# First modulation loads as eight row blocks, and keys that begin when all of shift and scale is there

## The chip, the cores and the metric

The kernel runs on one core of one Trainium2 chip. The metric is device time in microseconds (us) of one execution. The span that the profile shows runs from the first to the last instruction and is about 2 us shorter than that time. Every kernel has one profiled execution, so a number read from a trace is one sample.

## The reference

A transformer block with adaptive layer norm: 2048 tokens, width 1024. The part that matters is the beginning.

```python
mod = (_silu(c) @ w_mod).reshape(c.shape[0], 6, 1, -1)      # c: 1 x 1024, w_mod: 1024 x 6144, bf16
sa, ca, ga, sb, cb, gb = ...                                # six rows of 1024
h = _layernorm(x, axis=-1) * (1 + ca) + sa
x = x + ga * _A_ref(h, A_wqkv, A_wo)                        # linear attention: keys, values, queries from h
h = _layernorm(x, axis=-1) * (1 + cb) + sb
x = x + gb * _B_ref(h, ...)                                 # SwiGLU
```

The first keys need `h`, so they need the shift `sa` and the scale `ca`: two matrix-vector products ("matvecs") with the first 2048 columns of `w_mod`, 4.19 MB. Hidden unit 128 cc + p sits in chunk cc, partition p.

## The kernel before

x arrives in tiles of 128 tokens (256 KB). Shift (q = 0) and scale (q = 1) are loaded by halves b of the hidden units; the first half is enough for chunks 0 to 3, so the keys start on these while the second half is still loading.

```python
wme = [[big("wme", [DC, NB]) for _ in range(2)] for _ in range(2)]
def load_mod(b, q, lo, hi):
    nc.sync.dma_start(out=wme[b][q][:, :, lo:hi], in_=wm_v[:, :, q * D + b * NB + lo:q * D + b * NB + hi])
load_mod(0, 1, 0, NB)            # 1 MB in 1024 rows of 1 KB
load_mod(0, 0, 0, NB)
load_k(0); load_k(1); load_x(STC - 1, nc.sync); load_k(2); load_k(3)     # (shortened) 256 KB each
load_mod(1, 1, 0, NB)
load_mod(1, 0, 0, NB // 2)       # rows of 512 B
load_k(4); load_k(5)
load_mod(1, 0, NB // 2, NB)
load_k(6); load_k(7)
# ... cut ...
def mod_block(b, q, lo, hi):     # 128 columns by 128 rows at a time: a matmul with one moving column
    for i in range(lo, hi):
        col = q * DC + 4 * b + i
        for j in range(DC):
            mm(mod_ps[:, col:col + 1], lhsT=wme[b][q][:, j, i * P:(i + 1) * P],
               rhs=scT[:, j:j + 1], start=(j == 0), stop=(j == DC - 1))
    # ... copied to saT or, plus one, to ca1T
# ... cut: c, silu, layer norm and transposes of tiles 0 to 2, keep-warm matmuls in between ...
for lo, hi in ((0, 1), (1, 4)):
    mod_block(0, 0, lo, hi)
    for cc in range(lo, hi):
        modulate(hT, cc, ca1T, saT, 0, H)
k_mms(0, gs, accs, 0, 4)                  # 24 key matmuls: six groups, chunks 0 to 3
xn3 = ln1_norm(*ln1_stats(0, 3), dve=True)
pe_transpose_tile(hT, xn3, 3, DC // 2)    # ScalarE copies chunks 4 to 7 from PSUM, VectorE 0 to 3
for cc in range(4):
    modulate(hT, cc, ca1T, saT, H, SCW)
mod_block(1, 1, 0, 4)
# ... cut: keys of tile 3, the other half of the modulation and chunks 4 to 7, interleaved ...
```

`keep_warm(acc, n)` issues n matmuls of 512 columns whose result nobody reads, so that TensorE doesn't stand idle.

## Time and profile before

| | before |
|---|---|
| time, three executions | 839.66 us median (838.86 to 839.79) |
| span of the profiled execution (none of the three; it took 838.63 us) | 836.6 us |
| TensorE busy | 829.8 us (99%) |
| last modulation load that the first key needs has landed | 13.25 us |
| the first keys' own weights have landed | 13.94 us |
| first key matmul | 14.50 us |
| first value matmul ("V") | 31.95 us |

The page of the kernel before: the span, TensorE's busy time, and in 40 slices of 21 us TensorE's busy share and its granted clock (the share of full speed that the throttle allowed it) in tenths, the DMA share in tenths, and GB/s.

```profile
span 836.6 us, 11355 instructions
PE 829.8 (99%) x4701; PEld 380.7 (46%) x4701; DVE 307.6 (37%) x598; ACT 170.1 (20%) x255; POOL 60.9 (7%) x165
...
PE   8999999999999999999999999999999999999998
...
PEclk9999999999999999999999999999999999999999
DMA  9894890029997446337434173672505529710011
GB/s 311 305 253 100 254 213 2 13 68 239 366 243 262 151 151 207 120 99 229 150 102 151 45 221 100 201 239 62 189 1 127 188 69 322 241 60 0 13 64 51
```

TensorE bounds the kernel from the second slice on. DMA is near full in the first three slices and in some later ones, but there TensorE's digit stays at 9. From the start of the first V matmul to that of the last matmul of all, the trace has 801.32 us; with the same work after V, a saving before V should count one to one.

The chain of waits of the kernel before, for its first 60 us (start, us, what):

```profile
2.98 10.27 DMA wme<-in_w_mod_dram
...
13.30 0.37 PE mod_ps L98 x8
...
13.69 0.17 DVE saT L264
...
13.90 0.74 PE mod_ps L98 x24
14.64 5.20 PE acc L98 x24
```

The first keys wait for the second modulation load, then for matvecs, a copy and a modulation pass.

The timeline of TensorE in the same trace (start, us busy; in brackets the idle time before and what ended it):

```profile
14.50 5.34 PE L98 MATMUL acc<-wk,hT 128*128 128x512 bf16 x24
19.68 0.61 PE L101 MATMUL tp<-ident,xn 128*128 128x128 bf16 x8
20.13 0.94 PE L98 MATMUL mod_ps<-scT,wme 128*128 128x1 bf16 x32
21.78 0.61 PE L98 MATMUL acc<-wk,hT 128*128 128x512 bf16 x2 [0.71 <-DVE hT L218]
...
25.94 0.54 PE L98 MATMUL mod_ps<-scT,wme 128*128 128x1 bf16 x16
26.34 5.76 PE L98 MATMUL acc<-wk,hT 128*128 128x512 bf16 x25
```

The key stretch holds matvecs of the second half and a wait for tile 3. Its length, and the length of V, are in the windows view (from:to, length, busy time of each engine, then granted clock, DMA share and GB/s):

```profile
core 0: us, PE busy (x) PEld busy (x) DVE busy (x) ACT busy (x) POOL busy (x), PEclk, DMA share, GB/s
0.00:14.50 14.50, 11.99 (x119) 6.17 (x120) 7.54 (x20) 5.77 (x6) 3.13 (x12) 1.00 0.88 297
14.50:31.95 17.45, 16.51 (x143) 8.33 (x140) 8.83 (x28) 4.20 (x7) 2.17 (x35) 1.00 1.08 372
31.95:45.93 13.98, 13.98 (x66) 6.33 (x65) 10.90 (x28) 9.28 (x14) 3.22 (x8) 1.00 0.51 171
```

### The profile page before, as it was taken

The numbers are of one execution on the slowest core, as the hardware profiler recorded it, in microseconds if no ns is written. First come the engines' busy times: TensorE is split into PE (matmuls) and PEld (weight loads), VectorE is DVE, ScalarE is ACT, GpSimd is POOL, SyncE is SP. The second block draws the span as 40 slices with busy tenths as digits, with TensorE's granted clock in tenths as the row PEclk, the third lists the DMA queues.
The fourth block names the chain that finished last, engine by engine and source line by source line (L and its number), as shares of the span: only waits on it lengthen the run. The fifth ranks groups of instructions, "written<-read, shape, count | busy, mean of one in ns | idle before, by whom it ended". The sixth has DMA issues, their size and how long they took to land.

```text
span 836.6 us, 11355 instructions
## 1 busy us (share of the span) xinstructions
PE 829.8 (99%) x4701; PEld 380.7 (46%) x4701; DVE 307.6 (37%) x598; ACT 170.1 (20%) x255; POOL 60.9 (7%) x165
## 2 busy tenths in 40 slices
PE   8999999999999999999999999999999999999998
PEld 4444444444444444444444444444444444444444
DVE  5755554587413324521111344222114431111122
ACT  3455343334211111101111110111110101111000
POOL 2011211111130001100000010000001100000000
PEclk9999999999999999999999999999999999999999
DMA  9894890029997446337434173672505529710011
GB/s 311 305 253 100 254 213 2 13 68 239 366 243 262 151 151 207 120 99 229 150 102 151 45 221 100 201 239 62 189 1 127 188 69 322 241 60 0 13 64 51
DMA packets 127668, 129.34 MB, mean 155 GB/s; under 512 B 33920, under 2 KB 109184, under 8 KB 127104
## 3 DMA queue, kind: packets, MB, share of 16 engines
q1 hardware_dynamic: 123568, 115.36, 45.7%
q0 software_dynamic: 4048, 13.25, 5.4%
q8 instruction: 37, 0.61, 0.3%
q14 instruction: 15, 0.12, 0.1%
HBM read 108.53 MB, written 12.72 MB: 145 GB/s over the span
## 4 chain that ended last, share of the span: by engine, by line
PE 97%; DMA 1%; DVE 1%; SPq 0%; ACT 0%; issue 0%
PE acc L98 89%; PE a_ps L98 7%; DMA wme<-in_w_mod_dram 1%; PE kvp L98 1%; PE modr L98 0%; PE den L98 0%; PE mod_ps L98 0%; DVE hT L218 0%; SPq L120 0%; DVE wo L528 0%; PE wf L98 0%; DVE pq L273 0%; ACT eb L270 0%; ACT hT L226 0%; PE tp L101 0%
## 5 line engine op out<-in xcount | busy, mean ns | idle before, releaser
L98 PE MATMUL acc<-h2T,wgu 128*128 128x512 bf16 x1792 | 387.6, 379 | 0.0
L98 PEld LDWEIGHTS <-wgu 128*128 128x128 bf16 x1792 | 175.3, 98 | 211.3
L98 PE MATMUL acc<-wd,gu 128*128 128x512 bf16 (+2 forms) x924 | 196.1, 373 | 0.0
L597 DVE TENSOR_TENSOR gu<-acc,e 128x512 bf16<-128x512 f32 x112 | 77.5, 692 | 299.2 <-PE acc L98 296.5
L596 ACT ACTIVATE e<-acc 128x512 f32<-128x512 f32 x112 | 66.9, 597 | 374.8 <-PE acc L98 374.8
L98 PEld LDWEIGHTS <-gu 128*128 128x128 bf16 x924 | 89.3, 98 | 104.4
L98 PEld LDWEIGHTS <-hT 128*128 128x128 bf16 x512 | 49.2, 98 | 60.4 <-DVE hT L218 1.5
L618 DVE TENSOR_TENSOR e<-acc,gb_bc 128x512 f32<-128x512 f32 (+2 forms) x33 | 22.3, 675 | 131.9 <-PE acc L98 131.9
L98 PE MATMUL acc<-wk,hT 128*128 128x512 bf16 x256 | 57.6, 379 | 0.8 <-DVE hT L218 0.7
L98 PE MATMUL a_ps<-wo,pq 128*128 128x512 bf16 x256 | 57.4, 379 | 0.0
L98 PE MATMUL acc<-hT,wq 128*128 128x512 bf16 x256 | 56.8, 379 | 0.0
L98 PE MATMUL acc<-wv,hT 128*128 128x512 bf16 x256 | 55.9, 379 | 0.0
L270 ACT ACTIVATE eb<-acc 128x512 bf16<-128x512 f32 x64 | 37.9, 595 | 66.2 <-PE acc L98 63.1
L215 ACT ACTIVATE xn<-x,nmr,rstd 128x1024 bf16<-128x1024 f32 x16 | 19.8, 1240 | 126.3 <-POOL nmr L213 126.3
L565 POOL DMA_DIRECT2D x_scratch<-x x16 | 9.7, 608 | 418.5 <-DVE x L558 418.5
L98 PEld LDWEIGHTS <-pq 128*128 128x128 bf16 x256 | 25.0, 98 | 30.2
L98 PEld LDWEIGHTS <-wq 128*128 128x128 bf16 x256 | 24.6, 98 | 29.8 <-issue 0.9
L271 DVE TENSOR_SCALAR eb<-eb 128x512 bf16<-128x512 bf16 x64 | 18.4, 292 | 49.0 <-ACT eb L270 49.0
L558 DVE TENSOR_TENSOR x<-a_ps,x_sb 128x512 f32<-128x512 f32 x32 | 22.1, 691 | 7.9 <-PE a_ps L98 7.8
L199 POOL TENSOR_TENSOR rstd<-veps,neg_half 128x1 f32<-128x1 f32 x32 | 17.9, 559 | 75.3 <-DVE veps L197 72.9
L308 ACT CAST v<-acc 128x512 bf16<-128x512 f32 x32 | 18.3, 582 | 23.1 <-PE acc L98 23.0
L621 DVE TENSOR_TENSOR ob<-e,x1r 128x512 bf16<-128x512 f32 (+2 forms) x33 | 22.3, 675 | 1.0
(70 smaller groups left out, 263.1 us busy)
## 6 DMA issues: line engine op xcount, KB each, us to landing
wgu<-in_B_w_gate_dram SPq DMA_DIRECT2D x28, 1024.0 KB, 7.9
wgu<-in_B_w_up_dram SPq DMA_DIRECT2D x28, 1024.0 KB, 8.7
x_sb<-in_A_x_dram SPq DMA_DIRECT2D x32, 256.0 KB, 6.8
wml<-in_w_mod_dram SPq DMA_DIRECT2D x8, 1024.0 KB, 8.7
x_scratch<-x POOLq DMA_DIRECT2D x16, 512.0 KB, 3.0
x1r<-x_scratch SPq DMA_DIRECT2D x31, 256.0 KB, 2.8
wd<-in_B_w_down_dram SPq DMA_DIRECT2D x7, 1024.0 KB, 6.0
rbc<-rden_scratch POOLq DMA_DIRECT2D x16, 256.0 KB, 5.4
```

What stands on the lines that cost most here:

```text
L98: return tc.keep_in_program_order(nc.tensor.matmul(out, lhsT=lhsT, rhs=rhs, start=start, stop=stop))
L199: nc.gpsimd.tensor_tensor(out=rstd[:, 0:n], in0=veps[:, 0:n], in1=neg_half[:].to_broadcast([P, n]), op=ALU.pow)
L215: nc.scalar.activation(out=dst, in_=src, func=ACT.Identity, bias=nmr[:], scale=rstd[:, 0:1])
L270: nc.scalar.activation(out=e[:], in_=acc, func=ACT.Exp)
L271: nc.vector.tensor_scalar(out=e[:], in0=e[:], scalar1=1.0, scalar2=PHI_EPS, op0=ALU.min, op1=ALU.add)
L308: nc.scalar.copy(out=v[:, t * D + nb * NB:t * D + (nb + 1) * NB], in_=acc[:])
L558: nc.vector.tensor_tensor(out=x1[:, ns], in0=a_ps[:], in1=x_t[:, ns], op=ALU.add)
L565: nc.gpsimd.dma_start(out=x1_dram[st * P:(st + 1) * P, :], in_=x1[:])
L596: nc.scalar.activation(out=sg[:], in_=ps[0][:], func=ACT.Silu)
L597: gm = nc.vector.tensor_tensor(out=guT[sc][f // GPT][:, f % GPT, :], in0=ps[1][:], in1=sg[:], op=ALU.mult)
L618: nc.vector.tensor_tensor(out=yt, in0=y_ps, in1=gb_bc[:, ns], op=ALU.mult)
L621: nc.vector.tensor_tensor(out=ob, in0=yt, in1=x1r, op=ALU.add)
```

## The change

The intent: load `w_mod` by blocks of 128 rows with 4 KB in a row, which moves faster than rows of 1 KB and 512 B; accumulate the matvecs block by block under the loads, so that only the last block is exposed; and then run the keys without matvecs between them. The price is that 4.19 MB instead of 2.10 MB stand ahead of the first key.

```diff
-    wme = [[big("wme", [DC, NB]) for _ in range(2)] for _ in range(2)]
-    ... load_mod, and its calls between the key loads
+    wme = [big("wme", [2, 2 * D]) for _ in range(DC // 2)]
+    for j in range(DC):
+        nc.sync.dma_start(out=wme[j // 2][:, j % 2, :], in_=wm_v[:, j, 0:2 * D])
+    for cc in range(4):
+        load_k(cc)
     load_x(STC - 1, nc.sync)
+    for cc in range(4, DC):
+        load_k(cc)
...
+    def mod_block(j):
+        for col in range(2 * DC):
+            mm(mod_ps[:, col:col + 1], lhsT=wme[j // 2][:, j % 2, col * P:(col + 1) * P], rhs=scT[:, j:j + 1],
+               start=False, stop=(j == DC - 1 and col == 2 * DC - 1))
...
+        mm(mod_ps[:, 0:2 * DC], lhsT=ident[:], rhs=base[:], start=True, stop=False)   # shift 0, scale 1
...
+        keep_warm(spare, 5)
+        mod_block(0)
+        ... blocks 1 to 4, with tiles 0 to 2 and keep-warm matmuls between them
+        for j in range(5, DC):
+            keep_warm(spare, 4)
+            mod_block(j)
+        nc.vector.tensor_copy(out=sca[:], in_=mod_ps[:, 0:2 * DC])
+        for cc in range(DC):
+            modulate(hT, cc, ca1T, saT, 0, H)
+        k_mms(0, gs, accs, 0, 6)
         xn3 = ln1_norm(*ln1_stats(0, 3), dve=True)
+        tp3 = pe_transpose_tile(xn3)
+        for cc in range(DC):
+            nc.vector.tensor_scalar(out=hT[:, cc, H:SCW], in0=tp3[:, cc, :], ...)     # modulated from PSUM
+        k_mms(0, gs, accs, 6, DC)
         gs7, accs7 = k_groups[6:7], [acc_b("acc")]
+        k_mms(0, gs7, accs7)
         gs8, accs8 = k_groups[7:8], [acc_b("acc")]
         k_mms(0, gs8, accs8)
```

More of the change, by code (lines that the diff above doesn't have):

```diff
@@ L127 @@
     wk = [big("wk", [4, D]), big("wk", [4, D])]
-    wme = [[big("wme", [DC, NB]) for _ in range(2)] for _ in range(2)]
-    def load_mod(b, q, lo, hi):
-        nc.sync.dma_start(out=wme[b][q][:, :, lo:hi], in_=wm_v[:, :, q * D + b * NB + lo:q * D + b * NB + hi])
+    wme = [big("wme", [2, 2 * D]) for _ in range(DC // 2)]
     def load_k(cc):
         nc.sync.dma_start(out=wk[cc // 4][:, cc % 4, :], in_=wqkv_v[:, cc, D:2 * D])
-    load_mod(0, 1, 0, NB)
-    load_mod(0, 0, 0, NB)
-    load_k(0)
-    load_k(1)
+    for j in range(DC):
+        nc.sync.dma_start(out=wme[j // 2][:, j % 2, :], in_=wm_v[:, j, 0:2 * D])
+    for cc in range(4):
+        load_k(cc)
     load_x(STC - 1, nc.sync)
-    load_k(2)
-    load_k(3)
-    load_mod(1, 1, 0, NB)
-    load_mod(1, 0, 0, NB // 2)
-    load_k(4)
-    load_k(5)
-    load_mod(1, 0, NB // 2, NB)
-    load_k(6)
-    load_k(7)
+    for cc in range(4, DC):
+        load_k(cc)
     def load_w(view, lo, name):
@@ L167 @@
     nc.vector.memset(neg_half[:], -0.5)
+    base = const.tile([P, 2 * DC], BF16, name="base")
+    nc.vector.memset(base[:, 0:DC], 0.0)
+    nc.vector.memset(base[:, DC:], 1.0)
     scT = const.tile([P, DC], BF16, name="scT")
     sc32 = const.tile([P, DC, 32], BF16, name="sc32")
-    saT = const.tile([P, DC], F32, name="saT")
-    ca1T = const.tile([P, DC], F32, name="ca1T")
+    sca = const.tile([P, 2 * DC], F32, name="sca")
+    saT, ca1T = sca[:, 0:DC], sca[:, DC:2 * DC]
     sbT = const.tile([P, DC], F32, name="sbT")
@@ L219, in modulate, with pe_transpose_tile @@
                                 scalar2=biasT[:, cc:cc + 1], op0=ALU.mult, op1=ALU.add)
-    def pe_transpose_tile(hT, xn, t, split):
+    def pe_transpose_tile(xn):
         tp = acc_b("tp", (DC, P), BF16)
@@ L224, in pe_transpose_tile @@
             transpose(tp[:, cc, :], xn[:, cc * P:(cc + 1) * P])
-        if split < DC:
-            nc.scalar.copy(out=hT[:, split:DC, t * P:(t + 1) * P], in_=tp[:, split:DC, :])
-        nc.vector.tensor_copy(out=hT[:, 0:split, t * P:(t + 1) * P], in_=tp[:, 0:split, :])
+        return tp
     hTs = {}
@@ L251, in ln1 @@
             ln1_norm(*ln1_stats(sc, t))
-    def mod_block(b, q, lo, hi):
-        for i in range(lo, hi):
-            col = q * DC + 4 * b + i
-            for j in range(DC):
-                mm(mod_ps[:, col:col + 1], lhsT=wme[b][q][:, j, i * P:(i + 1) * P],
-                   rhs=scT[:, j:j + 1], start=(j == 0), stop=(j == DC - 1))
-        cs = slice(4 * b + lo, 4 * b + hi)
-        src = mod_ps[:, q * DC + 4 * b + lo:q * DC + 4 * b + hi]
-        if q == 1:
-            nc.vector.tensor_scalar_add(out=ca1T[:, cs], in0=src, scalar1=1.0)
-        else:
-            nc.vector.tensor_copy(out=saT[:, cs], in_=src)
+    def mod_block(j):
+        for col in range(2 * DC):
+            mm(mod_ps[:, col:col + 1], lhsT=wme[j // 2][:, j % 2, col * P:(col + 1) * P], rhs=scT[:, j:j + 1],
+               start=False, stop=(j == DC - 1 and col == 2 * DC - 1))
     last_phi = [None]
@@ L425 @@
         mod_ps = acc_b("mod_ps")
-        mm(mod_ps[:, 0:DC], lhsT=c_sb[:], rhs=ident[0:DC, 0:DC], start=True, stop=True)
-        keep_warm(spare, 10)
-        nc.scalar.activation(out=scT[:], in_=mod_ps[:, 0:DC], func=ACT.Silu)
+        mm(mod_ps[:, 2 * DC:3 * DC], lhsT=c_sb[:], rhs=ident[0:DC, 0:DC], start=True, stop=True)
+        mm(mod_ps[:, 0:2 * DC], lhsT=ident[:], rhs=base[:], start=True, stop=False)
+        nc.scalar.activation(out=scT[:], in_=mod_ps[:, 2 * DC:3 * DC], func=ACT.Silu)
@@ L429 @@
         xns = [ln1_norm(*ln1_stats(0, t)) for t in range(3)]
-        pe_transpose_tile(hT, xns[0], 0, DC)
-        keep_warm(spare, 3)
-        pe_transpose_tile(hT, xns[1], 1, DC)
-        keep_warm(spare, 2)
-        mod_block(0, 1, 0, 4)
-        pe_transpose_tile(hT, xns[2], 2, DC // 2)
-        keep_warm(spare, 4)
-        for lo, hi in ((0, 1), (1, 4)):
-            mod_block(0, 0, lo, hi)
-            for cc in range(lo, hi):
-                modulate(hT, cc, ca1T, saT, 0, H)
-        k_mms(0, gs, accs, 0, 4)
@@ L442 @@
-        xn3 = ln1_norm(*ln1_stats(0, 3), dve=True)
-        pe_transpose_tile(hT, xn3, 3, DC // 2)
-        for cc in range(4):
-            modulate(hT, cc, ca1T, saT, H, SCW)
-        mod_block(1, 1, 0, 4)
-        gs7, accs7 = k_groups[6:7], [acc_b("acc")]
-        k_mms(0, gs7, accs7, 0, 2)
-        for cc in (4, 5):
-            mod_block(1, 0, cc - 4, cc - 3)
-            modulate(hT, cc, ca1T, saT)
-            if cc == 4:
-                k_mms(0, gs7, accs7, 2, 4)
-        k_mms(0, gs + gs7, accs + accs7, 4, 5)
@@ L455, with turn @@
-        k_mms(0, gs[0:4], accs[0:4], 5, 6)
-        mod_block(1, 0, 2, 4)
-        for cc in (6, 7):
-            modulate(hT, cc, ca1T, saT)
-        k_mms(0, gs[4:6] + gs7, accs[4:6] + accs7, 5, 6)
-        k_mms(0, gs + gs7, accs + accs7, 6, 8)
+        def turn(t):
+            tp = pe_transpose_tile(xns[t])
+            nc.vector.tensor_copy(out=hT[:, :, t * P:(t + 1) * P], in_=tp[:])
+        keep_warm(spare, 5)
+        mod_block(0)
+        keep_warm(spare, 2)
+        mod_block(1)
+        turn(0)
@@ new lines @@
+        keep_warm(spare, 1)
+        mod_block(2)
+        keep_warm(spare, 1)
+        turn(1)
+        keep_warm(spare, 2)
+        mod_block(3)
+        keep_warm(spare, 2)
+        turn(2)
+        mod_block(4)
+        for j in range(5, DC):
[5 more added lines that the diff above has]
+        k_mms(0, gs, accs, 0, 6)
+        xn3 = ln1_norm(*ln1_stats(0, 3), dve=True)
@@ L461 @@
+        tp3 = pe_transpose_tile(xn3)
+        for cc in range(DC):
+            nc.vector.tensor_scalar(out=hT[:, cc, H:SCW], in0=tp3[:, cc, :], scalar1=ca1T[:, cc:cc + 1],
+                                    scalar2=saT[:, cc:cc + 1], op0=ALU.mult, op1=ALU.add)
+        k_mms(0, gs, accs, 6, DC)
+        gs7, accs7 = k_groups[6:7], [acc_b("acc")]
+        k_mms(0, gs7, accs7)
         gs8, accs8 = k_groups[7:8], [acc_b("acc")]
```

## The prediction

> **What bounds the kernel now.** TensorE is busy 829.8 of 836.6 us (page, part 1); the chain of waits is 97% PE. In the V phase, from 31.95 us, the timeline shows a matmul every 0.217 us without a break. So the change, which touches only the first 32 us, pays only by letting V start earlier. Up to there DMA holds PE: the windows view shows DMA share about 1.0 from 7 to 35 us, and the chain has a 10.27 us wait for a modulation load that ends at 13.25 us. The first key matmul runs at 14.50 us; V starts 17.45 us later: 13.9 us of key matmuls, 1.9 of matvecs, 0.6 of transposes, about 1.1 of waits.
>
> **What the change does.**
> - Bytes ahead of the first key: x (0.79 MB) and 4.19 MB of modulation instead of 2.10: about 5.1 us more.
> - Row size: the trace's packet records have medians of 46 ns for 1 KB, 84 for 2 KB, 159 for 4 KB; on 16 engines 356, 390, 412 GB/s. This agrees with the Trainium skill, "DMA: Bandwidth & Descriptors", section "Why small descriptors are slow" (fixed overhead per packet; here about 8 ns). All 4.19 MB are 64 packets on each engine, 10.2 us, against about 12.3 in 1 KB and 512 B rows.
> - Skew: the landing semaphores show the first modulation load ending between 7.45 and 10.28 us, five engines late, and that lateness stays. SP's queue stood 3.7 us behind 1,024-row loads, with DMA share 0.78 at 4 to 6 us. Blocks of 128 rows should fill this dip and cut part of the skew.
> - Matvecs: the same 128 (about 0.45 us per 16). Seven blocks hide under loads; the last is exposed. With four keep-warm matmuls (0.95 us) a block is 1.4 us against 1.27 us of load, so PE may slip 0.1 us a block.
> - Key stretch after: 64 matmuls (13.9 us) and eight transposes (0.5 us), no matvec, no wait: a chunk of keys takes 1.3 us against 0.67 us per 256 KB load; tile 3 needs about 3 us of normalisation within the 7.8 us of 36 matmuls, and loses two copies.
> - Evacuation gets two groups of cover instead of one; off the path.
>
> **Sum.** x has landed on most engines at 4.6 us; plus 10.2 us of blocks, 14.8; receipt and remaining skew (0.4 to 2.5 us) say 1.3: last block at 16.1 us (15.0 to 17.3). Then 16 matvecs 0.4, copy and modulate 0.83 (measured from last matvec to first key): first key at 17.3 us. Plus 14.4: V at 31.7 us against 31.95, then the same work. The change moves 2.8 us of loading ahead of the keys and takes 3 us of matvecs and waits out of them: nearly a wash.
>
> **Predicted time:** 839.4 us, 8 in 10 between 838.0 and 840.9. Faster by over 2%: 0.005; within 2%: 0.99; slower: 0.005.
>
> **What would show it.** First key at 17.3 us; from there to V 14.4 us without idle; V start within 1.2 us of 31.95; over 380 GB/s from 4 us; 4 KB packets at 159 ns; last block at 16.1 us with skew under 2.8 us; clock 1.00 throughout; V and all later phases of equal length.
>
> **What would make it wrong.** Engines as late as before or later (first key at 18.5, 1 us slower); no skew (up to 1.3 us faster); blocks come unevenly, PE idles and the clock drops ("TensorE: Matmul & The Clock Gate", section "HAM oscillation": gaps over about 3.4 us; before, no gap is so long and the clock stays 1.00); tile 3 or a key load arrives late and the key stretch waits.

## The result

| | before | after |
|---|---|---|
| time, four executions each | 839.26 us median (838.16 to 839.79) | 839.61 us median (839.43 to 841.25) |
| ratio, 95% interval | | 1.001 (0.9993 to 1.0028) |
| span of the profiled execution | 836.6 us | 839.4 us |
| spans of the three others | | 837.6, 837.7, 837.8 us |

A ratio is the mean time of one kernel's fast runs over that of the other's of the same rounds, so it isn't quite the ratio of the medians quoted. The change is within 2%. The same kernel in a later session (experiment 1) came out at 839.6 against 838.04 us, ratio 1.0017 with an interval from 1.0005 to 1.003: slower, by about 1.5 us (1.4 by the ratio, 1.6 by the medians).

The page of the changed kernel:

```profile
span 839.4 us, 11369 instructions
PE 831.8 (99%) x4708; PEld 381.6 (45%) x4708; DVE 307.5 (37%) x597; ACT 168.8 (20%) x253; POOL 60.6 (7%) x165
...
DMA  9793990029999545527434174571504529710011
GB/s 346 268 242 89 274 202 13 3 76 211 348 252 271 177 151 188 138 77 250 150 101 151 41 217 107 192 247 56 195 1 138 177 69 322 236 63 0 16 60 51
```

TensorE is as busy as before. DMA moves 346 GB/s instead of 311 in the first slice, as intended. What came of it shows in the chain of waits:

```profile
6.05 11.40 DMA wme<-in_w_mod_dram
17.44 0.05 issue
17.49 0.57 PE mod_ps L98 x16
...
18.16 0.18 DVE sca L435
...
18.36 0.39 DVE hT L211
...
18.80 9.30 PE acc L98 x36
```

The last block lands at 17.44 us, and the first key runs at 18.80 us, 4.3 us later than before (its own weights landed at 18.10). The timeline of TensorE:

```profile
14.88 0.54 PE L98 MATMUL mod_ps<-scT,wme 128*128 128x1 bf16 x16
15.28 1.02 PE L98 MATMUL acc<-sel 128*128 128x512 bf16 x4
17.49 0.55 PE L98 MATMUL mod_ps<-scT,wme 128*128 128x1 bf16 x16 [1.19 <-DMA wme<-in_w_mod_dram]
18.80 9.30 PE L98 MATMUL acc<-wk,hT 128*128 128x512 bf16 x36 [0.76 <-DVE hT L211]
```

Thirty-six key matmuls took 9.30 us here, 0.258 us each, instead of 0.217. The clock tells why; the windows view:

```profile
0.00:18.80 18.80, 14.89 (x190) 8.34 (x191) 7.84 (x22) 6.36 (x6) 3.13 (x12) 0.98 0.91 341
18.80:34.43 15.63, 15.63 (x72) 7.07 (x73) 9.84 (x28) 3.37 (x6) 2.17 (x35) 0.91 1.05 386
34.43:48.41 13.98, 13.98 (x66) 6.35 (x65) 9.44 (x26) 9.50 (x13) 3.21 (x8) 1.00 0.35 86
```

The granted clock was 0.5 from 18.18 to 21.59 us, one piece of 3.41 us in the trace's clock records. It began 0.69 us after the end of the idle piece of 1.19 us; the second one, of 0.76 us from 18.04 to 18.80, lies mostly inside it. So keys ran at half rate from 18.80 to 21.59 us, which costs half of 2.79, 1.4 us: the first 36 took 7.94 us in the later trace of the same kernel (a_again), not 9.30. It belongs to this execution: the three others had a clock of 1.00 and spans 1.6 to 1.8 us shorter. V is 13.98 us long in both kernels, and from the first V matmul to the last matmul of all it is 801.33 us against 801.32, so all but about 0.3 us, which came after the last matmul, is decided before V.

The landing semaphores of the trace say when each of the 16 DMA engines finished its part of a load. The last two modulation blocks of the changed kernel, in us, sorted:

```
block 6: 14.07 14.11 14.13 14.14 14.18 14.21 14.33 14.38 14.39 14.41 14.45 14.49 14.56 14.61 14.62 14.65
block 7: 15.34 15.38 15.40 15.42 15.44 15.47 15.61 15.65 15.67 15.68 15.72 15.77 15.83 15.87 15.91 17.44
```

Fifteen engines have the last block at 15.91 us. One takes 1.5 us longer. In the packet records there is one packet of another kind just then: 16,384 bytes on the queue that the profile calls "instruction", at 14.22 us, which took 1.02 us. The page counts 37 such packets, and 9,416 TensorE matmuls and weight loads; at 256 to a packet that would be 36.8. The Trainium skill, "Runtime: NRT & Kernel Launch", section "Instruction fetch mechanics", says that an engine's instructions are refilled in blocks of 16 KiB, 256 instructions, over a DMA queue; the packets agree. That gave the main theory: TensorE's instruction fetch holds up one DMA engine, and in the changed kernel it falls just before the last block that the keys need. The rival: the lateness comes from the loads themselves.

### The profile page after: what moved, and what is told of

Same layout as the page of the kernel before. It is cut to its first block, busy times and chain, and to the rows that moved or that the text cites. A ratio compares the mean times of both kernels' runs of the same rounds, so it can differ in the third digit from the quotient of the medians.

```text
span 839.4 us, 11369 instructions
## 1 busy us (share of the span) xinstructions
PE 831.8 (99%) x4708; PEld 381.6 (45%) x4708; DVE 307.5 (37%) x597; ACT 168.8 (20%) x253; POOL 60.6 (7%) x165
## 3 DMA queue, kind: packets, MB, share of 16 engines
q0 software_dynamic: 4048, 13.25, 5.3%
## 4 chain that ended last, share of the span: by engine, by line
PE 97%; DMA 2%; DVE 0%; SPq 0%; ACT 0%; issue 0%; DVEq 0%
PE acc L98 89%; PE a_ps L98 7%; DMA wme<-in_w_mod_dram 1%; PE kvp L98 1%; DMA x_sb<-in_A_x_dram 0%; PE modr L98 0%; PE den L98 0%; DVE wo L514 0%; PE wf L98 0%; SPq L120 0%; DVE pq L256 0%; ACT eb L253 0%; PE mod_ps L98 0%; PE tp L101 0%; DVE hT L211 0%
```

## The experiments

Eleven kernels ran, in three sessions, each on another chip; each session has its own runs of the kernel before, which all ratios are taken against. All results passed the comparison with the reference.

### 1. The changed kernel again (a_again)

No edit but a blank line.

> The changed kernel once more (only a blank line added), for a second trace of its loads and for times in the same rounds as the next three. Theory (fixed cost: TensorE's instruction fetch of 1.0 us falls on one DMA engine before the last block; random: some engines start w_mod late, at 4 to 6 us, by another amount in each execution): fetch at 14.2 to 14.4 us, one engine that lands the keys' loads 1.5 us later than it landed block 6; last block at 17.0 to 17.6 us, whatever the start-up lateness; clean executions about 1.0 to 1.6 us over the kernel before. Rival (the last block of the first profile was a chance event): last landing at about 16 us, time equal to before.

Measured: 839.6 us against 838.04, ratio 1.0017 (1.0005 to 1.003). First key 18.75 us, V 33.02 us. The windows view of this trace, which has the clock at 1.00 throughout:

```profile
0.00:18.75 18.75, 15.59 (x191) 8.47 (x191) 7.85 (x22) 6.36 (x6) 3.12 (x12) 1.00 0.89 336
18.75:33.02 14.27, 14.27 (x73) 6.73 (x74) 9.74 (x28) 3.37 (x6) 2.17 (x35) 1.00 1.05 385
```

So the key stretch is 14.27 us, all of it busy. The last block landed at 17.22 us, about where it did in the first trace, but for another reason. Here block 0 was already spread from 5.94 to 8.32 us, and three engines stayed about 1.0 to 1.5 us behind the median from there on. The fetch came at 14.64 us. I measure its effect by the sum, over the 16 engines, of the landing times after the first engine's: it rose by 1.39 us from block 6 to block 7. But the engine hit was an early one, so the last landing didn't move. There are two sources of late engines, then: the start of the loads, and the fetch. The theory's range for the last block held (17.0 to 17.6 us); that the fetch sets it did not: in this trace the start does.

In this trace TensorE paces the blocks as well:

```profile
16.18 0.54 PE L99 MATMUL mod_ps<-scT,wme 128*128 128x1 bf16 x16
16.59 1.02 PE L99 MATMUL acc<-sel 128*128 128x512 bf16 x4
17.45 0.54 PE L99 MATMUL mod_ps<-scT,wme 128*128 128x1 bf16 x16
18.75 7.94 PE L99 MATMUL acc<-wk,hT 128*128 128x512 bf16 x36 [0.76 <-DVE hT L212]
```

Block 6 landed at 15.92 us and was used at 16.18, block 7 at 17.22 and was used at 17.45, because four keep-warm matmuls (0.89 us in the chain) and 16 matvecs (0.38 us) fill the 1.27 us between them. A TensorE that has once fallen behind the loads therefore doesn't catch up: it began the last block 0.05 us after its landing in the first trace, but 0.23 us here, 0.28 in a_fewer_pe, 0.29 in a_fewer_pe2 and 1.12 in a_more_pe. Fewer keep-warm matmuls were not tried.

### 2. Fewer TensorE instructions before the last block (a_fewer_pe)

```diff
     def mod_block(j):
+        if j < 4:
+            for _ in range(2):
+                mm(spare[:], lhsT=wme[j // 2][:, j % 2, 0:P], rhs=wme[j // 2][:, j % 2, 0:NB], start=True, stop=True)
+            return
```

The shift and scale are wrong. The comparison with the reference passed all the same, so it doesn't check these small values closely.

> Wrong result on purpose: blocks 0 to 3 are read by two wide matmuls each in place of 16 matvecs, which takes TensorE about as long with 112 fewer instructions before the last block; loads and the tail are those of the changed kernel. Theory (the last block comes 1.5 us late on one DMA engine because TensorE's instruction fetch, a packet of 16384 bytes that took 1.02 us at 14.22 us, ran on that engine, and the fetch comes with the count of TensorE instructions, near 256): the fetch moves to after 16 us, all 16 engines land the last block by about 15.9 us, first key at about 17.2 us instead of 18.8, V start about 31.6 us, 1.5 us faster than the clean executions of the changed kernel (838.0). Rival (the late engine is late from the load itself): last landing stays at about 17.4 us and the time does not change.

Measured: the fetch did move, to 18.11 us, and no engine fell back between blocks 6 and 7. But four engines at block 0 and six at block 7 were over 0.5 us behind the median, the last block landed at 16.96 us, and the first key came at 18.54 us. And the time was 842.35 us against 838.6, ratio 1.005 (1.0037 to 1.0064): a miss by 4 us. V began at 32.81 us, 0.2 us earlier than in a_again, so the loss lies after it. The timeline of TensorE around the first products of keys and values:

```profile
63.98 1.22 PE L98 MATMUL kvp<-v,pk 128*32 128x64 bf16 x128
65.14 0.39 PE L98 MATMUL acc<-wk,hT 128*128 128x512 bf16 x1
66.77 1.03 PE L98 MATMUL acc<-wk,hT 128*128 128x512 bf16 x4 [1.25 <-issue]
```

TensorE stood still with no wait that the profile shows ("issue"), after 128 matmuls and 128 weight loads in 1.2 us. The same happened at the second such product:

```profile
94.06 1.22 PE L98 MATMUL kvp<-v,pk 128*32 128x64 bf16 x128
96.98 1.67 PE L98 MATMUL acc<-wk,hT 128*128 128x512 bf16 x7 [1.69 <-DMA wml<-in_w_mod_dram]
```

The profile puts this wait down to a load that these matmuls do not read. In both places a fetch packet starts as the product starts: at 63.91 us for the one of 63.98, and at 94.31 for the one of 94.06. From the first V matmul to the last matmul this kernel needs 804.05 us, the changed kernel 801.33.

### 3. The instructions given back later (a_fewer_pe2)

```diff
     (as a_fewer_pe, and)
+        for _ in range(26):                      # ahead of the first keys, while VectorE modulates
+            mm(spare[:, 0:1], lhsT=sel[:, 0, :], rhs=sel[:, 0, 0:1], start=True, stop=True)
...
+        for _ in range(30):                      # ahead of the eighth key group
+            mm(accs8[0][:, 0:1], lhsT=sel[:, 0, :], rhs=sel[:, 0, 0:1], start=True, stop=True)
```

> Wrong values on purpose, as a_fewer_pe, but the 112 TensorE instructions are given back later as tiny matmuls: 26 while the first keys wait for VectorE, 30 (about 0.9 us) ahead of the eighth key group. So every instruction after the keys stands where it stands in the changed kernel. Theory 1 (the fetch comes with the instruction count): fetch after 16.5 us, no engine falls back between block 6 and block 7; first key 17.2 us if the engines start evenly, 18.5 if they start as in a_fewer_pe. Theory 2 (TensorE stood idle 1.4 us at 65 us and 1.7 us at 95 us in a_fewer_pe because the 112 missing instructions moved the fetches to just before the key-value products, which use up 256 instructions in 1.2 us): no such gaps here, V to end 801.3 us again instead of 804.05. Rival: gaps stay, because they come from the wrong values or from data.

Measured: fetch at 17.74 us; one engine 1.0 us late from block 0, none more at block 7; last block at 16.28 us, first key at 17.87 us. The sum of lateness then rises by 1.37 us at the fourth x tile, the first load to end after the fetch. As theory 1 said, the fetch came after 16.5 us and no engine fell back between blocks 6 and 7, though the first key came 0.7 us after the 17.2 named for an even start. Theory 2 holds as well: from V to the last matmul it is 801.33 us again, and the products run on without a gap:

```profile
64.06 1.22 PE L98 MATMUL kvp<-v,pk 128*32 128x64 bf16 x128
65.22 5.14 PE L98 MATMUL acc<-wk,hT 128*128 128x512 bf16 x23
```

So 112 instructions at one place moved 2.7 us at others. That the position in the instruction stream decides it is shown. That TensorE is short of instructions there is inferred from the packets' times, and these fit: in this kernel the products start at 64.06 and 92.95 us and the fetches at 65.64 and 94.34, 1.4 to 1.6 us after the start, when the products are over; in the kernel before, too, the fetches (65.99 and 93.65 us) come when the products are over.

V came at 32.89 us. Of that the 30 tiny matmuls take about 0.76 us (30.41 to 31.17 us in the timeline), which leaves 32.1, about 0.9 us less than a_again. That isn't the fetch: in a_again it moved no last landing. It is the start of the loads: block 0 was complete at 7.30 us here and at 8.32 there, and the last block at 16.28 and 17.22. The time, 840.0 us with ratio 1.0026 (1.0013 to 1.0039), is no better than the changed kernel's, and two of its five executions had spans of 839.0 and 838.9 us against 837.6 to 838.0 of the others. No time shows what the fetch before the last block is worth.

### 4. More TensorE instructions before the blocks (a_more_pe)

```diff
-    keep_warm(spare, 11)
+    keep_warm(spare, 6)
+    for _ in range(60):
+        mm(spare[:, 0:1], lhsT=sel[:, 0, :], rhs=sel[:, 0, 0:1], start=True, stop=True)
```

> The changed kernel with five keep-warm matmuls replaced by 60 tiny ones at the start, 110 TensorE instructions more before the blocks. Theory (the fetch comes with the count, at 242 to 305 instructions started in all traces so far): it moves from 14.2 to about 10 us, and one engine falls about 1.5 us back between two middle blocks (3 to 5) instead of before the last one; last landing still 17 to 17.5 us. Rival (the time since the start decides): fetch at 14.2 us again.

Measured in one look (840.98 us): the fetch moved to 12.06 us, not quite as far as said, with 269 TensorE instructions started; the sum of lateness rose by 1.34 us from block 4 to block 5 and stayed. Last landing 17.47 us. The time since the start does not decide when the fetch comes. TensorE began the last block at 18.59 us only, and the first key came at 19.89.

In the eight traces of the changed kernel and its variants the sum of lateness rose by 1.16 to 1.50 us at the first load that ended after the fetch:

| trace | fetch at, us | TensorE instructions started by then | load that shows the step | step, us |
|---|---|---|---|---|
| after | 14.22 | 305 | block 7 | 1.50 |
| a_warm | 14.36 | 267 | block 7 | 1.47 |
| a_again | 14.64 | 269 | block 7 | 1.39 |
| a_rows_1k | 16.59 | 268 | block 7 | 1.16 |
| a_more_pe | 12.06 | 269 | block 5 | 1.34 |
| a_fewer_pe | 18.11 | 268 | x tile 3 | 1.41 |
| a_fewer_pe2 | 17.74 | 322 | x tile 3 | 1.37 |
| a_keys_first | 15.54 | 215 | block 6 | 1.34 |

Five of the eight fetches come at 267 to 269 instructions; why the others come at 215, 305 and 322 is open, so the count is no sharp threshold. Between early blocks the sum also moves without a fetch (by +1.16 us in a_again and by -1.36 in a_more_pe, from block 3 to block 4), so the step of a_more_pe is the least certain; from block 4 on, apart from the steps of the table, it changes by less than 0.3 us from one block to the next in all but a_warm (0.4). And the step is that of one engine: the last landing of the load moved by 1.5 us in the first trace, by 1.0 in a_keys_first, by 0.25 in a_warm, and not at all in a_again, a_rows_1k and a_more_pe; in a_fewer_pe and a_fewer_pe2 the load is one that the first keys don't need.

### 5. Keep-warm matmuls in the gap (a_warm)

```diff
-            keep_warm(spare, 4)
+            keep_warm(spare, 9 if j == DC - 1 else 4)
             mod_block(j)
+        keep_warm(spare, 3)
```

> The changed kernel with nine instead of four keep-warm matmuls ahead of the last modulation block and three behind it, so that TensorE isn't idle while it waits (idle 1.2 us and 0.8 us in the profile of the changed kernel). Theory (the clock drop at 18.2 us in that profile came from this idleness, and it comes only in some executions): clock 1.00 in the profile, first key still at about 18.8 us, V start 33.2 us instead of 34.4, no execution as slow as 841; median as the changed kernel's clean executions, about 839.5. Rival (the drop has another cause): the clock falls to 0.5 at about 18 us again.

Measured: 840.58 us, ratio 1.0026 (1.0014 to 1.0038). The clock stayed at 1.00 in the trace and in three of the other four executions, 0.999 in the fifth. But the nine matmuls ran until about 18.2 us, while the block had landed at 17.15: TensorE was late by 1.0 us, the first key came at 19.50, and V at 33.77, both 0.75 us later than in a_again. The remedy for a loss of 1.4 us in one profiled execution cost all of them about 0.75 us, by the ratios as well (1.0026 against 1.0017). It doesn't show that idleness is the cause: a_again has no clock under 0.999 in five executions either, without the remedy. Half-rate pieces followed idle pieces of 1.04 us in b_t3 and 1.09 in b_short, too, but none followed 1.45 us in a_rows_1k or 1.25 and 1.69 in a_fewer_pe. What sets them off is open.

### 6. Rows of 1 KB in the new order (a_rows_1k)

```diff
-    wme = [big("wme", [2, 2 * D]) for _ in range(DC // 2)]
+    wme = [big("wme", [4, 2, NB]) for _ in range(DC // 2)]
...
-        nc.sync.dma_start(out=wme[j // 2][:, j % 2, :], in_=wm_v[:, j, 0:2 * D])
+        nc.sync.dma_start(out=wme[j // 2][:, :, j % 2, :], in_=wm_v[:, j, 0:2 * D].rearrange("p (g n) -> p g n", g=4))
```

> The changed kernel with each block of 512 KB stored in another order so that its loads run in rows of 1 KB instead of 4 KB; order, count and size of the loads and all compute stay. Theory (row size works through the packet time only, 46 against 159/4 = 40 ns per KB): the median engine lands the last block about 1.7 us later than 15.6, at 17.3 us, last with the instruction fetch at 18.8 us, time +1.5 us against the changed kernel. Rival (1 KB rows are what made five engines up to 2.8 us late in the kernel before): blocks land with a spread of over 1.5 us from the first on, last landing after 19.5 us, time +2.5 us or more.

Measured: 841.74 us, ratio 1.0041 (1.0028 to 1.0054), where a_again has 1.0017, each to the kernel before in its own rounds: about 2.0 us slower than the changed kernel (0.0024 of 839 us), though the two intervals just overlap; V came at 35.22 us, 2.2 later than in a_again. The median engine had the last block at 17.71 us, 0.4 us later than the theory said, and the last engine at 19.59. Blocks came 1.50 us apart instead of 1.28 to 1.30. By its landings the rival was met to the letter: block 0 spread over 2.8 us, and the last landing came after 19.5 us. But one engine was very late there, not five, and a_again and a_more_pe spread block 0 over 2.38 and 2.65 us with 4 KB rows, so the spread doesn't separate the two. The median engine does: row size works through the packet time, 47 ns for 1 KB in this trace against 159 ns for 4 KB. That part of the prediction held, and the 4 KB rows are a real gain of the change, of about 2 us.

### 7. The kernel before with smaller first loads (b_split)

```diff
-        nc.sync.dma_start(out=wme[b][q][:, :, lo:hi], in_=wm_v[:, :, q * D + b * NB + lo:q * D + b * NB + hi])
+        step = 2 if b == 0 else DC
+        for j in range(0, DC, step):
+            nc.sync.dma_start(out=wme[b][q][:, j:j + step, lo:hi],
+                              in_=wm_v[:, j:j + step, q * D + b * NB + lo:q * D + b * NB + hi])
```

> The kernel before, with its first two modulation loads of 1 MB issued as four loads of 256 KB each (two row blocks), rows still 1 KB. Theory (five engines fall behind because one load of 1024 rows spread over the whole of w_mod starts unevenly; smaller loads don't): the spread of the first loads falls under 1 us, the second modulation load is there at about 11.3 us instead of 13.25, first key at about 12.6 us instead of 14.5, but only part of the 1.9 us is kept (tile 3 and the second half of the modulation come later in the stretch): 0.5 to 1.9 us faster than before. Rival (it is the 1 KB rows or a start-up effect whatever the loads): five engines late by over 1.4 us again, time unchanged.

Measured: 838.0 us against 838.6, ratio 0.9995 (0.9983 to 1.0006). Two engines were still 1.3 us late; the last piece landed at 12.97 instead of 13.25 us, and the first key ran at 14.07. The 1,024-row loads are not what makes engines late. With a_rows_1k above, a start-up effect whatever the form of the load is what remains of the rival.

### 8. Keys' weights ahead of the modulation (a_keys_first)

```diff
+    for cc in range(2):
+        load_k(cc)
     for j in range(DC):
         nc.sync.dma_start(out=wme[j // 2][:, j % 2, :], in_=wm_v[:, j, 0:2 * D])
-    for cc in range(4):
+    for cc in range(2, 4):
```

> The changed kernel with the first two key loads ahead of the eight modulation blocks, to see what starts late at 4 to 6 us, where every trace so far has 1 to 5 engines behind by 0.6 to 2.8 us. Theory A (a start-up effect of the queue, whichever tensor follows x): the spread shows in the first key load already (over 0.8 us). Theory B (the modulation weights themselves): key loads land within 0.5 us, the spread appears with block 0. Either way the last block comes 1.3 us later than in the changed kernel, about 18.7 us; first key about 20 us, unless the fetch or the start-up decide otherwise.

Measured in one look (843.53 us, with two half-rate pieces from 11.72 to 18.55 us): the first key load already landed between 5.21 and 6.46 us, a spread of 1.25 us, and modulation block 0 between 7.64 and 9.23. Packets over 350 ns cluster where each tensor begins: nine of 2 KB between 4.25 and 4.5 us for the keys, ten of 4 KB between 6.0 and 7.0 us for the modulation (five more of 4 KB follow up to 8.8 us). Neither theory alone: here each newly begun tensor has its slow packets. But slow packets are not the whole of it: in the kernel before, five engines were late after the first modulation load, whose packets of 1 KB took at most 267 ns between 4 and 7 us. Which engines are hit, and by how much, differs from trace to trace. Why is open. The last block landed at 19.24 us, and the first key, with TensorE at half rate for 6.8 us, came at 22.44 instead of the 20 expected.

### 9 to 11. Parts of the change in the kernel before (b_t3, b_split_t3, b_short)

b_t3 takes over one part of the change alone, for tile 3:

```diff
-        pe_transpose_tile(hT, xn3, 3, DC // 2)
+        tp3 = acc_b("tp", (DC, P), BF16)
+        for cc in range(DC):
+            transpose(tp3[:, cc, :], xn3[:, cc * P:(cc + 1) * P])
+        nc.scalar.copy(out=hT[:, 4:DC, H:SCW], in_=tp3[:, 4:DC, :])
         for cc in range(4):
-            modulate(hT, cc, ca1T, saT, H, SCW)
+            nc.vector.tensor_scalar(out=hT[:, cc, H:SCW], in0=tp3[:, cc, :], scalar1=ca1T[:, cc:cc + 1],
+                                    scalar2=saT[:, cc:cc + 1], op0=ALU.mult, op1=ALU.add)
```

> The kernel before with one part of the change alone: for tile 3, VectorE writes its first four chunks modulated straight from PSUM in place of a copy and four in-place passes. Before, TensorE waits 0.71 us for these at 21.1 us and 0.3 us for VectorE after them. Theory (this wait is on the path): V starts 0.7 to 1.0 us earlier counted from the first key (16.5 to 16.8 us instead of 17.45), time about 0.8 us less. Rival (the next loads or the VectorE chain after it take the gain back): first key to V stays at 17.4 us.

Measured: 838.76 us against 838.04, ratio 1.0005 (0.9991 to 1.0018). From the first key to V 19.16 us, of which about 1.7 are a half-rate piece from 22.93 to 26.35 us; without it about 17.5, no gain. The timeline of the trace:

```profile
19.62 0.59 ACT L446 COPY hT<-tp 128x512 bf16<-128x512 bf16 x1 [7.09 <-PE tp L101]
...
20.24 1.10 DVE L448 TENSOR_SCALAR hT<-tp,ca1T,saT 128x128 bf16<-128x128 bf16 x4 [2.27 <-ACT hT L446]
...
21.40 0.60 PE L98 MATMUL acc<-wk,hT 128*128 128x512 bf16 x2 [1.04 <-DVE hT L448]
```

VectorE starts when ScalarE's copy of the other half has ended, and four passes from PSUM take 1.10 us.

b_split_t3 is this edit on top of b_split.

> The two parts that did no harm, together: the first two modulation loads of the kernel before in pieces of 256 KB (b_split: first key 14.07 instead of 14.50 us, time ratio 0.9995), and tile 3 written modulated from PSUM. Theory: they add: V start at about 30.7 us instead of 31.95, time 1.0 to 1.4 us under before, which is 0.12 to 0.17%. Rival: the second half of the modulation, whose loads are no earlier, holds the keys: V at 31.5 us, time unchanged.

Measured: 837.91 us against 838.04, ratio 1.0 (0.9988 to 1.0013). First key 13.77, V 31.25 us, 17.48 us apart: again nothing from tile 3.

b_short is b_split with tile 2 copied by VectorE alone (`pe_transpose_tile(hT, xns[2], 2, DC)`), and tile 3 as in b_t3 but with ScalarE's copy after VectorE's four passes.

> b_split (first modulation loads in pieces of 256 KB) with two waits shortened: tile 2 copied by VectorE alone, and tile 3 modulated by VectorE from PSUM before ScalarE copies the other half, since in b_t3 and b_split_t3 VectorE stood 2.27 us until ScalarE's copy of the same PSUM tile had ended and gained nothing. Theory (VectorE's wait for ScalarE is what ate the gain of b_t3): VectorE starts tile 3 at the end of the transposes, the 0.7 to 1.0 us idle of TensorE before the keys of tile 3 goes under 0.4 us, first key to V 16.9 us instead of 17.45, first key at 13.4 to 13.8 us; V at about 30.5 us; clean executions 1.0 us under before (ratio 0.9985 to 0.999). Rival (the loads of the second half hold the keys anyway): first key to V 17.4 us and the time of b_split.

Measured: 839.26 us against 838.92, ratio 1.0001 (0.9987 to 1.0014). First key 13.58, V 32.85 us, 19.27 us apart with a half-rate piece from 23.18 to 26.59 us; without its 1.7 us about 17.6, no gain. VectorE now starts at once, at 19.40 us, and is done at 20.5. Yet TensorE waits as long as ever:

```profile
19.40 1.10 DVE L450 TENSOR_SCALAR hT<-tp,ca1T,saT 128x128 bf16<-128x128 bf16 x4 [1.66 <-PE tp L101]
...
20.59 0.59 ACT L452 COPY hT<-tp 128x512 bf16<-128x512 bf16 x1 [9.89 <-DVE ca1T L265]
...
21.23 0.59 PE L98 MATMUL acc<-wk,hT 128*128 128x512 bf16 x2 [1.08 <-ACT hT L452]
```

It waits for the last reader of the transposed tile, now ScalarE. By the count of the code's PSUM tiles, the seventh key group can only have the one that tile 3 was transposed into: two of the pool's four hold key groups, one the modulation. The wait that I wanted to shorten is for that tile to come free, not for VectorE, and both theories missed it. No version beat the kernel before.

## Why the prediction was right or wrong

The predicted time, 839.4 us, was 0.2 us off the measured median of 839.61, and well within the range. The claim beneath it, a gain of about 0.3 us, was not right: the later rounds put the change at +1.5 us. That the number fits so well is luck: V came 1.3 us later than predicted, and the kernel before was 0.7 to 1.6 us faster in the later sessions (medians of 838.04 to 838.92 us) than in the three runs that the prediction started from, so the two errors nearly cancel.

- **Last block at 16.1 us (15.0 to 17.3): mis-sized.** It was 17.44 us, and 17.22 in a_again. The sum had x on most engines at 4.6 us, which held (4.75 and 4.64), then 10.2 us of blocks and 1.3 us of receipt and skew. The median engine was done at 15.67 and 15.78 us instead of 14.8: slow first packets (eleven of 4 KB took 531 to 946 ns between 4.2 and 4.5 us in the first trace), and blocks that came 1.30 and 1.35 us apart on average instead of 1.27. Then the skew: 1.77 and 1.44 us from the median engine to the last, where 1.3 stood for skew and receipt together; the fetch made it in the first trace, the start of the loads in a_again. These two terms are the whole error of 1.1 to 1.3 us.
- **"Blocks of 128 rows should ... cut part of the skew": not reliably.** In five of the first seven traces of the table block 0 ended about 1.6 us or more after the median engine, against 2.5 us for the first modulation load before; b_split and a_rows_1k show that neither size nor rows of the loads is the cause. And the prediction did not know the second source at all, the instruction fetch, although the packet records before had it: one at 17.40 us, where it moved no last landing.
- **Row size: right.** 4 KB packets at 159 ns, 401 to 426 GB/s from 7 to 15 us (from 4 to 5 us, though, 192 instead of the predicted 380 and more); a_rows_1k shows a worth of about 2 us. The Trainium skill, "DMA: Bandwidth & Descriptors", section "Why small descriptors are slow", which states a fixed overhead per packet, agrees.
- **From the last block to the first key 1.23 us: right**, 1.31 us from the matvec's start (17.49 to 18.80); in a_again TensorE's lateness makes it 1.53 us from the landing.
- **Key stretch of 14.4 us without idle: right.** 14.27 us in a_again, against 17.45 before.
- **Clock 1.00 throughout: wrong**, in one of four executions, and in the profiled one. Its warning was there, but tied to gaps of over 3.4 us, after the Trainium skill, "TensorE: Matmul & The Clock Gate", section "HAM oscillation". Here the clock fell after one of 1.19 us, and experiment 5 leaves the cause open. The kernel before seems to lose such a piece as well: 13 of its 29 executions in the three later sessions had a mean clock of 0.998, which over 836 us is the 1.7 us of one half-rate piece.
- **V at 31.7 us: wrong by 1.3 us** (33.02 in a_again; 34.43 with the slow clock). By trace, first key +4.25 us and key stretch −3.18 us make +1.07 us against the profiled kernel before; another 0.3 us lies between the last matmul and the end of the span (3.63 us in a_again, 3.34 before), unexplained.

The intended gain is there, then: faster rows, hidden matvecs, a key stretch 3.2 us shorter. It is paid for by 2.10 MB more ahead of the first key and by waiting for the last of 16 engines on all of it. What made that engine late, the start of the loads or the instruction fetch in that window, differs from trace to trace.

## What to carry to other kernels

A start that waits for many loads waits for the slowest of 16 DMA engines, so estimate it from the last landing, not from bytes over bandwidth, and expect the lateness of an engine to stay, by and large, for the loads queued behind (before: the last engine 2.4 us after the median at 13.25 us, 2.2 at 25.51). Count the program's own instructions among the loads: one fetch per some 256 TensorE instructions cost one engine 1.2 to 1.5 us here, which counts when that engine becomes the last, and a change in instruction count here can open a gap somewhere else. An estimate that ends within 0.3 us of no change, from terms that vary by 1 us, says "no change"; it does not say which sign.

## What the Trainium skill lacked or had wrong

- "DMA: Bandwidth & Descriptors" does not say what an instruction fetch does to data on the same engine: here a 16 KB packet took 1.02 us, and the summed lateness of the loads rose by 1.16 to 1.50 us in eight traces of eight.
- "Runtime: NRT & Kernel Launch", section "Instruction fetch mechanics", calls the fetch hidden by the issue rate. In a_fewer_pe TensorE stood idle 1.25 and 1.69 us just after 256 instructions in 1.2 us, and not in a_fewer_pe2, which has the same instructions at those places and 112 more ahead of them; that the fetch is what it lacked is inferred.
- "TensorE: Matmul & The Clock Gate", section "HAM oscillation", gives gaps of over about 3.4 us as what to avoid. Here 3.41 us at half clock came with no such gap: the idle pieces before it were of 1.19 us (after), 1.04 (b_t3) and 1.09 (b_short).
- "DMA: Bandwidth & Descriptors", section "Where 436 GB/s comes from", lets about 358 GB/s bind loads from HBM, while it gives 425 GB/s as measured for 16 MB. Here the windows of the changed kernel have 401 to 426 GB/s from 7 to 15 us, on one core with rows of 4 KB, so the first figure did not bind.
- No page has the slow first packets of a newly begun tensor, up to 946 ns for 4 KB (after, at 4.39 us) against a median of 159 ns, nor engines that fall behind at the start of a tensor's loads, by up to 2.8 us (before, first modulation load, 7.45 to 10.28 us).
